# Attention with a mixture of experts: on VectorE, a tile's division moves behind the masked maxima of its tick, and the gate's bias is added one tick later

## The chip, the core and the metric

One program runs on one core of a Trainium2 chip. Its engines each work through their own list of instructions in order and wait for one another by semaphores: TensorE (PE in the rows; PEld is its weight load), VectorE (DVE), ScalarE (ACT), GpSimd (POOL) and SyncE (SP), which issues most DMAs. The metric is the device time of one execution in microseconds (us).

## The reference

The kernel computes block-sparse attention over 4 batches, 8 heads and 768 positions of 64 features, and then a mixture of 8 experts over the 3072 tokens that come out:

```python
scores = scale * np.matmul(q, k.transpose(0, 1, 3, 2))
# mask: neighbour blocks, first and last block, 3 sampled blocks a row of blocks
scores = np.where(mask, scores, -1000000000.0)
scores = scores - np.max(scores, axis=-1, keepdims=True)
attn = np.exp(scores)
attn = attn / (np.sum(attn, axis=-1, keepdims=True) + 1e-09)
...
logits = x @ w_gate + modality_bias[modality_id]
e_idx = np.argmax(logits, axis=1)
...
h = np.maximum(x[mask] @ w1[e], 0.0)
out[mask] = gate_w[mask, None] * (h @ w2[e])
```

## The kernel before

The work has two parts. The attention part (to about 226 us) makes 24 tiles of 128 token rows, `xr`; the experts' part multiplies groups of 256 rows that went to one expert, with every operand split into two fp32r halves, and keeps TensorE at it to the end.

A loop over ticks writes the attention part, and the program's order on every engine is the order in which this loop writes it. An item is a quarter of a sparse tile (two batches, two block rows of 32 queries), or a head pair of the dense first and last blocks ("d" items, which see all 768 keys). In tick `t` each step of `ORDER` is done for the item that is `LAG` ticks old:

- S: score products on TensorE (L557; dense L401), two PSUM banks that hold for two items
- M: masked maxima on VectorE, two custom instructions with a short read each (L565); dense: two plain maxima and a small one (L414 to L417)
- X: exponentials on ScalarE (L573; dense L423, L424)
- T and A: transposes on TensorE (L582; dense L433), copied out by ScalarE (L587; dense L440)
- W and V: products with the shared and with the own values (L604; L597 and L613), once a tile; dense L451
- O: `divide` on VectorE, once a tile, which reads V's two banks: add (L458), reciprocal (L459), multiply 128x512 (L460). It gives the tile's two banks back
- Y: transposes of the finished tile (L620), copied by ScalarE (L622)
- G: `gate`, the product with the gate's weights (L630), and on VectorE the add of the bias, `lg` (L633), behind which `end_tile` puts the routing of two tiles on a list, `fillers`

A sparse tile has four items, so TensorE's long steps fall on two ticks of four. Between the steps `hook(0)` to `hook(7)` take small work from lists: the routing (argmax, softmax weight, rank in the expert: L315 to L390, some 25 VectorE instructions of 0.15 to 0.25 us for two tiles), the choice of the first two groups, loads of the first experts' weights and their split (L752 on ScalarE, L755 on VectorE). The eight PSUM banks come from one pool. The line that matters:

```python
ORDER = 'OXTSMGVAYW'
```

So O is written first in its tick, ahead of M, and the bias is added in G's tick, right behind M.

Of the kernel before, what the change touches and what calls it, by code (L numbers as in the profile page):

```python
# [21 lines left out]
B, H, S, D = 4, 8, 768, 64  # L22
# [34 lines left out]
START_TICKS = 14  # L57
DENSE_DVE = ((0, 0), (0, 1))
DENSE_AFTER = (21, 29, 45, 47)
LAG = {'d': {'S': 0, 'M': 1, 'X': 2, 'T': 4, 'A': 4, 'W': 7, 'O': 8, 'V': 101, 'Y': 11, 'G': 13}, 's': {'S': 0, 'M': 1, 'X': 2, 'T': 4, 'A': 4, 'W': 5, 'V': 7, 'O': 8, 'Y': 10, 'G': 13}}  # L60
ORDER = 'OXTSMGVAYW'
ADVANCE = (((2, 3), (6, 6), (7, 1)), ((0, 2), (1, 1), (6, 4)))
LHS = (6, 5)
LHS_DVE = (True, True)
# [26 lines left out]
def attention_moe(ctx, tc, kD, qD, qH, v0, v1, blocks, modality, w_gate, bias, w1, w2, out):  # L91
# [30 lines left out]
    with ExitStack() as actx:  # L122
# [5 lines left out]
        def bank():  # L128
            return psum.tile([P, 512], F32, name="bank")
# [495 lines left out]
        def gate(tau, xT):  # L625
            tp = bank()
            for pr in range(NPAIR):
                for j in range(2):
                    r = slice(64 * j, 64 * j + 64)
                    nc.tensor.matmul(tp[r, 0:E], lhsT=xT[:, pr, r], rhs=wg_raw[:, pr, :], start=pr == 0, stop=pr == NPAIR - 1, tile_position=(0, 64 * j))  # L630
            if tau - tau % 2 not in lgs:
                lgs[tau - tau % 2] = small.tile([P, 2, E], F32, name="lg")
            nc.vector.tensor_tensor(lgs[tau - tau % 2][:, tau % 2, :], tp[:, 0:E], btok[:, tau, :], ALU.add)  # L633
# [596 lines left out]
        xrs, turns, banks, sums, ats, gated, written = {}, {}, {}, {}, {}, set(), {}  # L1230
# [5 lines left out]
        def tau_of(m, half):  # L1236
            return half * (NT // 2) + m + 1

        def end_tile(m, half):
            tau = tau_of(m, half)  # L1240
            gate(tau, turns.pop((m, half)))
            gated.add(tau)
            if tau ^ 1 in gated:
                t = tau - tau % 2
                fillers.append(routing(t, lgs.pop(t), [xrs.pop((t % (NT // 2) + n - 1, half)) for n in range(2)]))
# [9 lines left out]
        NI = len(items)  # L1255
# [6 lines left out]
        def hook(place):  # L1262
            for f in work_at.pop((t, place), []):
                f()
            if t < NI:
                ph = 0 if t < at["s", 1, 0, 0, 0] else 1
                for at_, k in ADVANCE[ph]:
                    if place == at_:
                        advance(k)
                for at_, k in CHOOSE:  # L1270
                    if place == at_:
                        step(choosers, k)
                for at_, k in EARLY:
                    if place == at_:
                        step(early, k)
                if place == LHS[ph] and slots_todo:
                    slot_lhs(nc.vector if LHS_DVE[ph] else nc.gpsimd)
# [41 lines left out]
        for g in range(2 * NM):  # L1319
            half, m = divmod(g, NM)  # L1320
            t = at["s", half, m, 0, 0]
# [21 lines left out]
        def do(op, it):  # L1343
            if (op, it) in done:
                return
            done.add((op, it))
            if it[0] == "d":
                _, b, pr = it
                half = b // HB
                if op == "S":  # L1350
                    if pr % 2 == 0:
                        for c, o in enumerate(dense_scores(b, pr)):
                            st["d", b, pr + c] = o
                elif op == "M":
                    st[it] = dense_max(b, pr, *st[it])
                elif op == "X":
                    st[it] = dense_exp(b, pr, *st[it])
                elif op == "T":
                    st[it] = dense_transpose(b, pr, *st[it])
                elif op == "A":  # L1360
                    st[it] = dense_copy(b, pr, *st[it])
                elif op == "W":
                    st[it] = dense_weigh(b, pr, *st[it])
                elif op == "O":
                    if (b % HB, pr) == (0, 0):
                        new_tile(-1, half)
                    dense_out(b, pr, *st.pop(it))
                elif (b % HB, pr) == (HB - 1, NPAIR - 1):
                    if op == "Y":
                        turns[-1, half] = turned(xrs[-1, half])  # L1370
                    elif op == "G":
                        end_tile(-1, half)
            else:
                _, half, m, n, b = it
                if op == "S":
                    if b == 0:
                        sp = scores(qraw[m, half], half * NM + m, n)
                        for b_ in range(HB):
                            st["s", half, m, n, b_] = sp
                elif op == "M":  # L1380
                    st[it] = masked(m, n, b, st[it])
                elif op == "X":
                    if (n, b) == (0, 0):
                        sums[m, half] = small.tile([P, 4, 2], F32, name="sums", bufs=4)
                    st[it] = exps(sums[m, half][:, 2 * b + n, :], *st[it])
                elif op == "T":
                    st[it] = transposed(n, st[it])
                elif op == "A":
                    if n == 0:
                        ats[m, half, b] = work.tile([P, 16, 2, 32], F32, name="at", bufs=NAT)  # L1390
                    copied(n, b, st.pop(it), ats[m, half, b])
                    if (n, b) == (1, HB - 1):
                        sums[m, half] = spread(sums[m, half])
                elif (n, b) == (1, HB - 1):
                    if op == "W":
                        st[it] = bank()
                        weigh_shared(half * NM + m, st[it], [ats[m, half, b_] for b_ in range(HB)])
                    elif op == "V":
                        banks[m, half] = bank()
                        sum_rows(sums.pop((m, half)), banks[m, half])  # L1400
                        weigh_own(half * NM + m, st[it], [ats[m, half, b_] for b_ in range(HB)])
                    elif op == "O":
                        new_tile(m, half)
                        divide(st.pop(it), banks.pop((m, half))[:, 0:H], slice(0, P), H, xrs[m, half][:, 0:HD])
                    elif op == "Y":
                        turns[m, half] = turned(xrs[m, half])
                    elif op == "G":
                        end_tile(m, half)

        man = tc.manual_schedule(engines=MAN) if MAN else ExitStack()  # L1410
        with man:
            constants()
            for token in START:
                op, at_ = token[0], tuple(int(c) for c in token[1:] if c.isdigit())
                if token[:2] == "SP":
                    spare(int(token[2:]))
                elif op == "h":
                    t = int(token[1:])
                    for spot in range(8):
                        hook(spot)  # L1420
                elif op.isupper():
                    do(op, ("d" if len(at_) == 2 else "s", *at_))
                elif token == "tb":
                    spare()
                else:
                    loads[token]()
            t = START_TICKS
            while t < NI + LAG["s"]["G"] + 1 or fillers or slots_todo or choosers or early:
                spot = 0
                for op in ORDER:  # L1430
                    if op in "TSMAXOW":
                        hook(spot)
                        spot += 1
                    for kind in "ds":
                        k = t - LAG[kind][op]
                        if 0 <= k < NI and items[k][0] == kind:
                            do(op, items[k])
                hook(7)
                if t >= NI:
                    tail[0], tail[1] = t >= NI + TAIL, t >= NI + LAG["s"]["V"]  # L1440
                    for _ in range(2):
                        advance(2)
                        while slots_todo:
                            slot_lhs(nc.vector if len(slots_todo) % 2 else nc.gpsimd)
                        step(choosers, 1)
                        step(early, 1)
                t += 1

        hp, op, xp = [bank() for _ in range(4)], [bank() for _ in range(2)], [bank() for _ in range(2)]
# [59 lines left out]
```

## Time and profile before

| | us |
|---|---|
| median of 3 runs (lowest, highest) | 521.74 (521.41, 523.24) |
| the profiled execution | 523.66 |
| its span, first to last instruction | 521.9 |
| TensorE busy in the span | 499.5 |
| VectorE, ScalarE, GpSimd busy | 388.4, 335.5, 244.9 |

The profiled execution is 1.9 us above the median, and its time 1.8 above its span. Busy times of TensorE are of pipelined instructions: of two neighbours the next begins some 0.07 us before the modelled end of the first, so an idle time that a row shows is somewhat shorter than the time lost.

### The profile page before, as it was taken

The numbers are of one execution on the slowest core, as the hardware profiler recorded it, in microseconds if no ns is written. First come the engines' busy times: TensorE is split into PE (matmuls) and PEld (weight loads), VectorE is DVE, ScalarE is ACT, GpSimd is POOL, SyncE is SP. The second block draws the span as 40 slices with busy tenths as digits, with TensorE's granted clock in tenths as the row PEclk, the third lists the DMA queues.
The fourth block names the chain that finished last, engine by engine and source line by source line (L and its number), as shares of the span: only waits on it lengthen the run. The fifth ranks groups of instructions, "written<-read, shape, count | busy, mean of one in ns | idle before, by whom it ended". The sixth has DMA issues, their size and how long they took to land.

```text
span 521.9 us, 18958 instructions
## 1 busy us (share of the span) xinstructions
PE 499.5 (96%) x7124; PEld 420.6 (81%) x7124; DVE 388.4 (74%) x1136; ACT 335.5 (64%) x765; POOL 244.9 (47%) x514
## 2 busy tenths in 40 slices
PE   7999999989899999899999999999999999999995
PEld 5667776767778777688989798998989899898974
DVE  5886688686689899967986868667686766768573
ACT  3799787978789978844545655555565545655561
POOL 6779685576458884312275051323324222241423
PEclk9999999999999999999999999999999999999999
DMA  8997885999756778965878797879669696877860
GB/s 293 332 249 227 241 222 184 244 228 258 196 174 191 207 219 245 273 192 200 242 281 294 246 297 258 266 233 301 200 240 284 227 295 202 280 223 251 260 209 25
DMA packets 59063, 123.84 MB, mean 237 GB/s; under 512 B 9681, under 2 KB 17618, under 8 KB 58962
## 3 DMA queue, kind: packets, MB, share of 16 engines
q1 hardware_dynamic: 54704, 108.88, 68.7%
q0 software_dynamic: 4256, 13.65, 7.9%
q8 instruction: 58, 0.95, 0.8%
q14 instruction: 43, 0.35, 0.3%
q10 hardware_dynamic: 2, 0.00, 0.0%
HBM read 105.97 MB, written 12.86 MB: 228 GB/s over the span
## 4 chain that ended last, share of the span: by engine, by line
PE 73%; DMA 11%; DVE 7%; ACT 3%; SPq 2%; issue 2%; POOL 0%; DVEq 0%; POOLq 0%; ACTq 0%
PE bank L810 8%; PE bank L812 8%; PE bank L811 8%; PE bank L827 7%; PE bank L826 7%; PE bank L825 7%; PE bank L557 6%; PE bank L582 6%; DMA slot<-x_d,gi 5%; PE bank L604 3%; PE bank L613 3%; PE bank L451 2%; DMA slot<-w 2%; PE bank L630 2%; PE bank L401 2%
## 5 line engine op out<-in xcount | busy, mean ns | idle before, releaser
L755 DVE TENSOR_TENSOR slot<-slot 128x1024 fp32r<-128x1024 f32 x99 | 124.6, 1272 | 63.1 <-ACT slot L752 54.9
L752 ACT CAST slot<-slot 128x1024 fp32r<-128x1024 f32 x104 | 107.0, 1047 | 68.3 <-PE bank L811 49.5
L810 PE MATMUL bank<-slot 128*128 128x256 f32 x384 | 108.4, 282 | 0.2 <-issue 0.2
L812 PE MATMUL bank<-slot 128*128 128x256 f32 x384 | 107.9, 281 | 0.1
L811 PE MATMUL bank<-slot 128*128 128x256 f32 x384 | 107.6, 280 | 0.0
L573 ACT ACTIVATE a<-y,mn 128x256 f32<-128x256 f32 x176 | 88.7, 511 | 7.9 <-DVE mn L565 7.7
L846 POOL DMA_INDIRECT out<-slot,si x20 | 27.3, 1364 | 109.5 <-ACT slot L842 106.5
L827 PE MATMUL bank<-slot 128*128 128x512 f32 x192 | 75.9, 395 | 0.4 <-DVE slot L818 0.4
L826 PE MATMUL bank<-slot 128*128 128x512 f32 x192 | 75.9, 395 | 0.0
L825 PE MATMUL bank<-slot 128*128 128x512 f32 x192 | 75.8, 395 | 0.0
L810 PEld LDWEIGHTS bank<-slot 128*128 128x128 f32 x384 | 72.3, 188 | 0.6
L811 PEld LDWEIGHTS bank<-slot 128*128 128x128 f32 x384 | 72.2, 188 | 0.6
L812 PEld LDWEIGHTS bank<-slot 128*128 128x128 f32 x384 | 72.2, 188 | 0.3 <-DVE slot L755 0.3
L565 DVE CUSTOM_DVE_ANT_1 y<-bank,smask 128x256 f32<-128x256 f32 x176 | 66.2, 416 | 0.5 <-PE bank L557 0.3
L502 POOL COPY slot<-slot 128x128 f32 x264 | 63.6, 293 | 0.0
L527 POOL TENSOR_SCALAR slot<-slot 32x1024 f32<-32x1024 f32 x40 | 41.7, 1042 | 33.2 <-issue 12.8
L587 ACT COPY at<-bank 128x512 f32<-128x512 f32 x88 | 50.6, 576 | 9.0 <-PE bank L582 9.0
L582 PE MATMUL bank<-ident,a 128*128 128x128 f32 x352 | 52.1, 280 | 3.0 <-issue 2.2
L557 PE MATMUL bank<-slot,q_raw 64*32 64x256 f32 x1408 | 48.7, 382 | 0.0
L582 PEld LDWEIGHTS bank<-ident,a 128*128 128x128 f32 x352 | 38.1, 141 | 7.3 <-issue 2.3
L827 PEld LDWEIGHTS bank<-slot 128*128 128x128 f32 x192 | 36.1, 188 | 9.2 <-DVE slot L818 0.9
L826 PEld LDWEIGHTS bank<-slot 128*128 128x128 f32 x192 | 36.0, 188 | 8.3 <-DVE slot L755 0.4
(307 smaller groups left out, 859.8 us busy)
## 6 DMA issues: line engine op xcount, KB each, us to landing
slot<-w SPq DMA_DIRECT2D x100, 512.0 KB, 5.2
slot<-v SPq DMA_DIRECT2D x180, 128.0 KB, 4.0
x_d<-xr SPq DMA_DIRECT2D x22, 256.5 KB, 4.2
q_raw<-qH SPq DMA_DIRECT2D x22, 256.0 KB, 4.8
slot<-v SPq DMA_DIRECT2D x16, 256.0 KB, 5.1
slot<-slot SPq DMA_DIRECT2D x120, 32.0 KB, 4.4
slot<-kD SPq DMA_DIRECT2D x13, 256.0 KB, 3.6
slot<-v SPq DMA_DIRECT2D x4, 768.0 KB, 12.4
```

The source lines that it names most:

```text
L557: nc.tensor.matmul(sp[u][32 * pr:32 * pr + 32, b * 256:(b + 1) * 256], lhsT=q[r, b * NPAIR + pr, n, :], rhs=kv[r, s0:s0 + 8, b, pr, :], st ...
L565: nc.vector.tensor_tensor_reduce(y[:, u, :].rearrange("p (s f) -> p s f", s=8), sp[u][:, b * 256:(b + 1) * 256].rearrange("p (s f) -> p s ...
L573: nc.scalar.activation(a[:, u, :], y[:, u, :], AF.Exp, bias=mn[:, u:u + 1], scale=-1.0, accum_out=total[:, u:u + 1])
L582: nc.tensor.transpose(tp[:, k:k + P], a[:, u, c * P:(c + 1) * P], ident)
L752: nc.scalar.copy(h, s)
L755: (eng or (nc.gpsimd if n in POOL_SPLITS else nc.vector)).tensor_tensor(l, s, h.bitcast(F32), ALU.subtract)
L810: nc.tensor.matmul(o, lhsT=h[:, fs], rhs=xh[g % 2][:, c, :], start=c == 0 and f % 2 == 0, stop=False)
L811: nc.tensor.matmul(o, lhsT=h[:, fs], rhs=xl[g % 2][:, c, :], start=False, stop=False)
L812: nc.tensor.matmul(o, lhsT=l[:, fs], rhs=xh[g % 2][:, c, :], start=False, stop=c == 3 and f % 2 == 1)
L825: nc.tensor.matmul(o, lhsT=hh[0][:, f, ts_], rhs=h[:, fs], start=f == 0, stop=False)
L826: nc.tensor.matmul(o, lhsT=hh[0][:, f, ts_], rhs=l[:, fs], start=False, stop=False)
L827: nc.tensor.matmul(o, lhsT=hl[f // 4][:, f % 4, ts_], rhs=h[:, fs], start=False, stop=f == 7)
```

## The change

O goes behind M in the tick's order. The gate's step is cut in two: G keeps the product, and a new step L, one tick older, adds the bias (in the last ticks, from `NI` on, L follows G at once). The hooks keep their places beside the other steps. The routing of a pair of tiles therefore starts one tick later.

```diff
-LAG = {'d': {'S': 0, 'M': 1, 'X': 2, 'T': 4, 'A': 4, 'W': 7, 'O': 8, 'V': 101, 'Y': 11, 'G': 13}, 's': {'S': 0, 'M': 1, 'X': 2, 'T': 4, 'A': 4, 'W': 5, 'V': 7, 'O': 8, 'Y': 10, 'G': 13}}
-ORDER = 'OXTSMGVAYW'
+LAG = {'d': {'S': 0, 'M': 1, 'X': 2, 'T': 4, 'A': 4, 'W': 7, 'O': 8, 'V': 101, 'Y': 11, 'G': 13, 'L': 14}, 's': {'S': 0, 'M': 1, 'X': 2, 'T': 4, 'A': 4, 'W': 5, 'V': 7, 'O': 8, 'Y': 10, 'G': 13, 'L': 14}}
+ORDER = 'XTSMLOGVAYW'
...
                     nc.tensor.matmul(tp[r, 0:E], lhsT=xT[:, pr, r], rhs=wg_raw[:, pr, :], start=pr == 0, stop=pr == NPAIR - 1, tile_position=(0, 64 * j))
+            return tp
+
+        def logits(tau, tp):
             if tau - tau % 2 not in lgs:
...
+        def gate_tile(m, half):
+            gates[m, half] = gate(tau_of(m, half), turns.pop((m, half)))
+
         def end_tile(m, half):
             tau = tau_of(m, half)
-            gate(tau, turns.pop((m, half)))
+            logits(tau, gates.pop((m, half)))
...
                     elif op == "G":
+                        gate_tile(m, half)
+                        if t >= NI:
+                            do("L", it)
+                    elif op == "L":
                         end_tile(m, half)
...
                 spot = 0
+                hook(spot)
                 for op in ORDER:
-                    if op in "TSMAXOW":
+                    if op in "TSMAXW":
+                        spot += 1
                         hook(spot)
-                        spot += 1
```

VectorE at the first tick of the loop in which a dense item's maxima stand with a division (62 to 67 us in the profile), before:

```order
L458 TENSOR_SCALAR rt<-bank 128x8
L459 RECIPROCAL rt<-rt 128x8
L460 TENSOR_TENSOR xr<-bank,rt 128x512
L414 TENSOR_REDUCE nm_1823<-bank 128x1
L415 TENSOR_REDUCE nm_1823<-bank 128x1
L417 TENSOR_SCALAR nb__1826<-nm_1823 128x1
L591 TENSOR_TENSOR rexp<-sums,quad 128x32
```

and with the change:

```order
L414 TENSOR_REDUCE nm_1818<-bank 128x1
L415 TENSOR_REDUCE nm_1818<-bank 128x1
L417 TENSOR_SCALAR nb__1821<-nm_1818 128x1
L458 TENSOR_SCALAR rt<-bank 128x8
L459 RECIPROCAL rt<-rt 128x8
L460 TENSOR_TENSOR xr<-bank,rt 128x512
L591 TENSOR_TENSOR rexp<-sums,quad 128x32
```

The division went behind the three instructions of the dense maxima. The second place is VectorE at the next such tick (84 to 89 us), before:

```order
L633 TENSOR_TENSOR lg<-bank,btok 128x8
L315 TENSOR_REDUCE mx<-lg 128x2
L458 TENSOR_SCALAR rt<-bank 128x8
L459 RECIPROCAL rt<-rt 128x8
L460 TENSOR_TENSOR xr<-bank,rt 128x512
L318 TENSOR_TENSOR dl<-lg,mx 128x16
L323 SCALAR_TENSOR_TENSOR eq<-dl,desc 128x16
L326 TENSOR_REDUCE first<-eq 128x2
L414 TENSOR_REDUCE nm_2425<-bank 128x1
L415 TENSOR_REDUCE nm_2425<-bank 128x1
L417 TENSOR_SCALAR nb__2428<-nm_2425 128x1
```

and with the change (L636 is the add of the bias):

```order
L414 TENSOR_REDUCE nm_2409<-bank 128x1
L415 TENSOR_REDUCE nm_2409<-bank 128x1
L417 TENSOR_SCALAR nb__2412<-nm_2409 128x1
L636 TENSOR_TENSOR lg<-bank,btok 128x8
L458 TENSOR_SCALAR rt<-bank 128x8
L459 RECIPROCAL rt<-rt 128x8
L460 TENSOR_TENSOR xr<-bank,rt 128x512
L591 TENSOR_TENSOR rexp<-sums,quad 128x32
L315 TENSOR_REDUCE mx<-lg 128x2
L318 TENSOR_TENSOR dl<-lg,mx 128x16
L323 SCALAR_TENSOR_TENSOR eq<-dl,desc 128x16
L326 TENSOR_REDUCE first<-eq 128x2
```

Here the maxima overtake the bias, the division and four instructions of the routing. The third place is VectorE near the end of the attention part (212 to 216 us), where the second group's rows are chosen (L1115 to L1122), before:

```order
L565 ISA mn 128x1
L1115 TENSOR_TENSOR hb<-oh,ce_5987 128x144
L1119 TENSOR_SCALAR off<-cm_5985,cm_5258 128x1
L1122 TENSOR_SCALAR rh__6105<-rhi,off 128x18
L458 TENSOR_SCALAR rt<-bank 128x8
L459 RECIPROCAL rt<-rt 128x8
L460 TENSOR_TENSOR xr<-bank,rt 128x512
L565 ISA y,mn<-bank,smask 128x256
```

and with the change:

```order
L565 ISA mn 128x1
L458 TENSOR_SCALAR rt<-bank 128x8
L459 RECIPROCAL rt<-rt 128x8
L460 TENSOR_TENSOR xr<-bank,rt 128x512
L591 TENSOR_TENSOR rexp<-sums,quad 128x32
L565 ISA y,mn<-bank,smask 128x256
```

The choice of rows, which now begins a tick later, no longer stands ahead of the last items' maxima.

## Rows read from the trace of the kernel before

**Rows 1.** Busy time by stretch: from:to, length, then PE, PEld, DVE, ACT, POOL (instructions), PEclk, DMA.

```profile
150.00:183.00 33.00, 33.00 (x918) 25.90 (x916) 29.34 (x145) 30.35 (x101) 26.43 (x80) 1.00 0.71 200
183.00:226.00 43.00, 39.44 (x1048) 31.21 (x1046) 38.82 (x191) 33.70 (x99) 21.86 (x43) 1.00 0.84 243
...
260.00:474.00 214.00, 213.57 (x1371) 193.09 (x1371) 153.12 (x188) 116.41 (x143) 72.50 (x79) 1.00 0.80 259
```

**Rows 2.** VectorE's waits, whole span: what waited, for whom, us, times, longest.

```profile
DVE rt L458 <- PE bank L597: 11.4, 8, 2.6
DVE lg L633 <- PE bank L630: 9.8, 12, 1.6
...
DVE xr L460 <- PE bank L613: 6.6, 13, 0.7
```

**Rows 3.** TensorE's groups, 30 to 226 us: busy, mean ns, idle before and who ended it.

```profile
L582 PE MATMUL bank<-ident,a 128*128 128x128 f32 x349 | 51.7, 280 | 3.0 <-issue 2.2 <-ACT a L423 0.5 <-ACT a L573 0.3
...
L604 PE MATMUL bank<-slot,at 128*64 128x64 f32 x704 | 26.8, 225 | 4.4 <-issue 2.9 <-ACT at L587 1.4
...
L451 PE MATMUL bank<-slot 128*64 128x64 f32 x240 | 9.0, 226 | 0.5 <-DVE mn L565 0.5
L433 PE MATMUL bank<-ident,a 128*128 128x128 f32 x48 | 7.2, 280 | 1.8 <-issue 1.5 <-ACT a L423 0.4
...
L597 PE MATMUL bank<-rexp,fold 128*32 128x8 f32 x176 | 5.5, 187 | 0.4 <-ACT at L587 0.4
```

**Rows 4.** Timeline of VectorE, first dense tick: start, length, instruction, idle before it.

```profile
63.68 0.17 DVE L458 TENSOR_SCALAR rt<-bank 128x8 f32<-128x8 f32 x1 [2.55 <-PE bank L597]
...
64.62 0.69 DVE L460 TENSOR_TENSOR xr<-bank,rt 128x512 f32<-128x512 f32 x1 [0.54 <-PE bank L613]
65.23 0.68 DVE L414 TENSOR_REDUCE nm<-bank 128x1 f32<-128x512 f32 x1
...
66.41 0.48 DVE L591 TENSOR_TENSOR rexp<-sums,quad 128x32 f32<-128x32 f32 x1
```

**Rows 5.** Timeline of ScalarE, same tick.

```profile
66.58 0.69 ACT L423 ACTIVATE a<-bank,nb__1826 128x512 f32<-128x512 f32 x1 [0.85 <-DVE nb__1826 L417]
```

**Rows 6.** Timeline of TensorE, same tick.

```profile
61.91 1.52 PE L401 MATMUL bank<-slot,qd 64*64 64x512 f32 x16
...
63.45 1.08 PE L613 MATMUL bank<-slot,at 128*32 128x64 f32 x64
...
65.48 1.09 PE L557 MATMUL bank<-slot,q_raw 64*32 64x256 f32 x32
...
67.46 0.94 PE L604 MATMUL bank<-slot,at 128*64 128x64 f32 x24 [0.32 <-issue]
```

**Rows 7.** Timeline of VectorE, second dense tick.

```profile
84.61 0.17 DVE L633 TENSOR_TENSOR lg<-bank,btok 128x8 f32<-128x8 f32 x1 [1.41 <-PE bank L630]
...
85.75 0.69 DVE L460 TENSOR_TENSOR xr<-bank,rt 128x512 f32<-128x512 f32 x1 [0.46 <-PE bank L613]
...
87.22 0.68 DVE L414 TENSOR_REDUCE nm<-bank 128x1 f32<-128x512 f32 x1
```

**Rows 8.** Timeline of TensorE, second dense tick.

```profile
89.40 0.66 PE L582 MATMUL bank<-ident,a 128*128 128x128 f32 x4 [0.54 <-ACT a L423]
...
91.36 0.44 PE L433 MATMUL bank<-ident,a 128*128 128x128 f32 x2 [0.37 <-ACT a L423]
```

**Rows 9.** Timeline of VectorE, one sparse tick: the maxima of an item and what follows.

```profile
180.00 0.41 DVE L565 CUSTOM_DVE_ANT_1 y<-bank,smask 128x256 f32<-128x256 f32 x1
...
180.68 0.21 DVE L591 TENSOR_TENSOR rexp<-sums,quad 128x32 f32<-128x32 f32 x1
```

**Rows 10.** Timeline of VectorE where the experts' part begins.

```profile
224.40 0.69 DVE L804 TENSOR_TENSOR slot<-bank,slot 128x512 fp32r<-128x512 f32 x1 [2.55 <-ACT slot L803]
...
228.59 2.35 DVE L755 TENSOR_TENSOR slot<-slot 128x1024 fp32r<-128x1024 f32 x2
```

**Rows 11.** Timeline of VectorE: two casts of one shape in the routing.

```profile
111.88 0.17 DVE L380 CAST rlo<-r 128x4 f32<-128x4 int32 x1
111.95 1.03 DVE L381 CAST rhi<-r 128x4 f32<-128x4 int32 x1
```

More of the change, by code (lines that the diff above doesn't have):

```diff
@@ L1237, in tau_of @@
             return half * (NT // 2) + m + 1
+        gates = {}
+        def gate_tile(m, half):
+            gates[m, half] = gate(tau_of(m, half), turns.pop((m, half)))
         def end_tile(m, half):
             tau = tau_of(m, half)
-            gate(tau, turns.pop((m, half)))
+            logits(tau, gates.pop((m, half)))
             gated.add(tau)
@@ L1371, in do @@
                     elif op == "G":
+                        gate_tile(-1, half)
+                    elif op == "L":
                         end_tile(-1, half)
@@ L1407, in do @@
                     elif op == "G":
+                        gate_tile(m, half)
+                        if t >= NI:
+                            do("L", it)
+                    elif op == "L":
                         end_tile(m, half)
```

## Prediction, made before the changed kernel ran

> **What bounds the kernel now.** I read the busy times by stretch first, because an average over the span hides that there are two parts. From 260 us on TensorE is busy 213.57 of 214 us; nothing that VectorE does there is changed, so a gain or loss can only be made before, and is carried to the end as it is. In the attention part TensorE is busy 33.00 of 33 us (150 to 183) and 39.44 of 43 (183 to 226), VectorE 29.34 and 38.82 [rows 1]: TensorE is the bound, with VectorE close behind it, closest in the second stretch.
>
> Then I read the waits of both engines. VectorE waits 11.4 us for V's sums before the division, 6.6 us for V's products inside it and 9.8 us for the gate's product before the bias, 27.8 us in all [rows 2]. That is what the change goes at, and most of it is worth nothing: while VectorE waits there, TensorE works. What can be won is TensorE's own idle time, 30 to 226 us. Of it, 6.6 us in the rows shown have only "issue" as releaser, which no order on VectorE touches; 3.5 us end with an instruction of ScalarE or VectorE (0.5 and 0.3 at L582, 1.4 at L604, 0.5 at L451, 0.4 at L433, 0.4 at L597) [rows 3]. These 3.5 us, with what "issue" hides of the same cause, are the ceiling.
>
> **The change part by part.** No instruction is added or removed; it is a matter of who stands behind whom.
>
> *Dense ticks.* Last I read the three ticks in which dense maxima meet a division. In the first, VectorE stands idle 2.55 us, begins the division at 63.68, waits 0.54 us more inside it, and only then, at 65.23, begins the maxima, though the dense products ended at 61.91 + 1.52 = 63.43 [rows 4, 6]. ScalarE waits 0.85 us for the maxima and exponentiates at 66.58 [rows 5]; TensorE's W, at 67.46, has 0.32 us of idle before it [rows 6]. The row says "issue", but W begins 0.2 us behind the first exponential's end (66.58 + 0.69 = 67.27), which I take to be the reader of the bank that W writes. The third such tick (120 to 126) repeats this with 0.30 us. In the second, bias, division and routing all stand ahead, the maxima begin at 87.22, and TensorE loses 0.54 and 0.37 us to the exponentials [rows 7, 8]. With the maxima first, the exponentials come 1.6 us earlier or more, which is over every one of these gaps: 0.32 + 0.30 + 0.54 + 0.37 = 1.5 us, bounds 0.9 (the two gaps named by the rows) and 1.5.
>
> *The other waits named.* The 0.5 us at L451 wait for maxima behind a long piece of the rank's work, which now starts a tick later: I take it whole, bounds 0 and 0.5. The rest, 1.4 + 0.4 + 0.3 = 2.1 us [rows 3], lies mostly between 183 and 226 us, where VectorE has no slack. There the maxima now overtake a division (1.2 us from L458 to the next instruction when it needn't wait: 65.23 - 63.68 less 0.54, and some 0.2) and, for the last items, the choice of the second group's rows. But ScalarE's copies also stand behind its own weight casts, which stay. I take half, 1.0, bounds 0 and 2.1. Since an idle row is shorter than the time lost by some 0.1 us, six gaps gone give 0.6 more (bounds 0 and 0.8). Gain: 1.5 + 0.5 + 1.0 + 0.6 = 3.6 us.
>
> *What is late next: the division.* In a sparse tick the maxima take 180.68 - 180.00 = 0.68 us [rows 9], then 0.4 us of small instructions stand before the multiply. V on TensorE lasts 1.08 [rows 6], and the maxima's scores are done before V begins: the maxima fit into the wait for V, and the division ends as now, or up to 0.3 us later. This cover is worth nothing where VectorE is already late (183 to 226), and there TensorE's next need of the two banks decides. In a dense tick the cover is short: the dense maxima take 66.41 - 65.23 = 1.18 us. From 63.43 they end at 64.6, the small instructions at 65.0, the multiply at 65.7; now it ends at 64.62 + 0.69 = 65.31, and the score products S, whose second bank is the division's in the built program before and after, begin at 65.48, 0.17 us behind it [rows 4, 6]. So S is held some 0.4 us, twice (bounds: 0, if the first maximum may start before the last dense product, and 0.65, if it starts 0.25 late). In the second tick the maxima end between 85.3 and 85.8, as their products are done before the 84.61 of the bias [rows 7]; the multiply starts between 85.75 and 86.2: 0.2 us, bounds 0 and 0.45. Loss 1.0, bounds 0 and 1.75.
>
> *The bias one tick later.* What waits behind it on VectorE is only the routing, 20 to 30 small instructions a pair of tiles that nobody needs soon. The gate's bank is held a tick longer; the pool gives it out later for that, and the built program has its next user over 2 us of TensorE's work away. On SyncE's queue four stores of finished rows move a tile later and the halves of the first weights a tick later; on GpSimd's the gathers keep their place ahead of the same work. Their cover is that five buffers of rows go round; without it a division would wait for a store to land. Cost 0, bounds 0 and 0.5.
>
> *The start of the experts.* From 224.40 to the weights' splits at 228.59, VectorE runs without a gap behind its 2.55 us wait [rows 10], and TensorE soon needs the first of these splits. With the routing later, a few of its instructions move from ahead of 224 into this stretch: 0.3 us, bounds 0 and 0.6 (seven small instructions).
>
> **Sum.** 3.6 - 1.0 - 0.3 = 2.3 us less: the profiled execution's 523.66 (span 521.9) would become 521.3. It lay 1.9 us above the median of the timed runs; the same 2.3 us off the median 521.74 give **519.4 us**. With the bounds of the terms it is 516.8 (gains 4.9, no loss) to 523.7 (gains 0.9, losses 2.85).
>
> **A rule weighed.** Two casts of one shape, next to each other, take 0.17 and 1.03 us [rows 11], so the routing's small instructions can cost six times their usual, and a tick's shift changes which of them do. The Trainium skill (SBUF — State Buffer, "Who interferes with whom") says that VectorE's copies, casts and tensor-scalars can need a port pair that GpSimd shares, and that the second to issue is blocked for the whole of the other's instruction. By the row alone the shift costs nothing on average; by the rule it could put such an instruction ahead of maxima that were free of it, which is the last rival.
>
> **The rivals.**
> *Nothing is won* (521.0 to 522.5): the removed gaps come back. For it: TensorE has 6.6 us of idle that nobody named releases, S held by the division takes up to 1.75, and only 3.5 us were there to win. Against it: three ticks show the maxima late by a wait that the new order cannot have.
> *The stretch of 183 to 226 is VectorE's* (517): all 3.5 us and the hidden 0.8 go and S is not held, 4.3 to 4.9 us less. For it: VectorE's 38.82 of 43 us there. Against it: ScalarE's casts.
> *Slower, by the division's banks*: if the dense maxima cannot start before VectorE's division would now have ended, S waits the whole 1.18 - 0.17 = 1.0 us in three ticks, and where VectorE is late each of some six tiles from 183 to 226 gives its banks back 0.68 us later, against a TensorE that I give no slack there: 3.0 + 4.1, less the 3.6 gained: 525.2. It decides once divisions end over 0.2 us later than now in the dense ticks and over half a microsecond in the late ones. For it: the 0.17 us of [rows 4, 6]; against it: in two of the three ticks VectorE stands idle before.
> *The collisions*: the shift makes five rounds of late routing longer by 0.9 us each (1.03 less 0.17), half of it felt by TensorE: 2.2 us, so 521.6.
>
> **Chances.** My forecast (517.8 to 520.8) 0.50; nothing won 0.20; VectorE's stretch 0.13; slower by the banks 0.10; collisions 0.07. A measurement of this kernel tells about 0.5% (2.6 us) from no change. Below 519.1: a little under half of the forecast and all of the third, 0.36. Above 524.4: the fourth case, 0.10. Within: 0.54. The range is 517.0 to 523.0: below it lies about half of the third case, above it the fourth and little else.
>
> **What the changed profile would show.** Right: VectorE's waits for V and for the gate fall from 27.8 us to under 15; in the three dense ticks the dense maxima begin within 0.3 us of the dense products' end and W and the transposes after them have no gap; TensorE's idle time named for ScalarE and VectorE falls from 3.5 to about 1.5 us, with new idle at S (L557) of under 1.5. Wrong: idle at S over 2 us, VectorE's waits moved to the maxima instead of gone, TensorE's start into the experts (first L810) not about 2 us earlier, or other "issue" gaps than now, which would move the time by as much as the whole forecast without a cause in the change.

## The result, and the profile after

The changed kernel took **529.18 us**, the median of 6 runs (525.1 to 531.4), against 521.70 of 6 runs of the kernel before on the same chip. The ratio on record is 1.0101, 95% interval 1.0063 to 1.0139; the two medians by themselves stand at 1.0143. So it is slower by 1% or somewhat more, where 519.4 was forecast with a range of 517.0 to 523.0. On a second chip it was 528.43 against 523.98 (1.0083, 1.0049 to 1.0118); the kernel before differs by up to 4.5 us between chips, so only kernels of one chip are compared below. Ratios and means leave out the runs that are more than 1.5% above the fastest of their kernel: 5 of 12 in the second measurement of the division alone, 9 of 35 of the kernel before on one chip, 4 of 35 or fewer elsewhere.

The profiled execution took 525.1 us (span 523.4). It is the fastest of the six and only 1.4 us above the profiled execution of the kernel before; a second profile, of a run of 529.81 us, follows under the experiments. The busy times of the first by stretch, to be read against [rows 1] (the last number is what the DMA engines moved, in GB/s):

```profile
150.00:183.00 33.00, 32.45 (x898) 25.67 (x900) 27.71 (x132) 28.68 (x96) 25.85 (x71) 1.00 0.72 203
183.00:226.00 43.00, 37.93 (x974) 29.62 (x954) 35.71 (x183) 31.20 (x93) 19.81 (x41) 0.96 0.85 232
...
260.00:474.00 214.00, 213.17 (x1391) 192.49 (x1391) 155.74 (x190) 115.76 (x142) 72.77 (x79) 1.00 0.78 255
```

From 260 us on TensorE is as busy as before. From 183 to 226 TensorE is busy 1.5 us less, VectorE 3.1 us less, and the granted clock is 0.96 on average where it was 1.00.

VectorE's waits, against [rows 2], and TensorE's between 30 and 226 us, against [rows 3]:

```profile
DVE y L565 <- ACT a L573: 8.7, 6, 3.4
DVE r L363 <- PE bank L353: 8.6, 7, 3.0
...
DVE y L565 <- PE bank L557: 5.8, 6, 2.2
...
DVE xr L460 <- PE bank L613: 1.5, 4, 0.5
...
DVE lg L636 <- PE bank L630: 0.7, 1, 0.7
```

```profile
PE bank L604 <- issue: 2.8, 3, 2.3
PE bank L433 <- issue: 2.8, 1, 2.8
PE bank L604 <- POOL slot L488: 1.1, 1, 1.1
PE bank L604 <- ACT at L587: 0.6, 2, 0.4
PE bank L613 <- issue: 0.6, 1, 0.6
PE bank L557 <- DVE lg L636: 0.5, 1, 0.5
PE bank L582 <- DVE rt L458: 0.5, 1, 0.5
PE bank L582 <- ACT a L573: 0.4, 1, 0.4
PE bank L1147 <- DVE hoh L1137: 0.4, 1, 0.4
PE bank L620 <- DVE xr L460: 0.4, 1, 0.4
PE bank L620 <- DVE mn L565: 0.2, 1, 0.2
```

The waits for V and the gate, 27.8 us, are down to 2.2 (1.5 + 0.7): the edit does what it says. But VectorE now waits at the maxima instead (8.7 + 5.8) and at the rank (8.6); it is ahead, and ScalarE and TensorE set its pace. TensorE's idle time that an engine's name ends went from 3.5 to 4.1 us. The "issue" idle time hardly changed as a sum, 7.1 before (2.9 + 2.2 + 1.5 + 0.5) and 6.4 now with the row of 0.2 that is left out, but two stops of 2.8 and 2.3 us make up most of it.

The timelines of the first dense tick, VectorE's first dense maxima and then TensorE, show the gain that was forecast, against [rows 4] and [rows 6]:

```profile
61.33 0.69 DVE L414 TENSOR_REDUCE nm<-bank 128x1 f32<-128x512 f32 x1 [2.33 <-PE bank L401]
```

```profile
60.21 1.52 PE L401 MATMUL bank<-slot,qd 64*64 64x512 f32 x16
...
63.78 1.09 PE L557 MATMUL bank<-slot,q_raw 64*32 64x256 f32 x32
64.80 0.64 PE L630 MATMUL bank<-wg_raw,xT 128*64 128x8 f32 x16
65.29 1.52 PE L604 MATMUL bank<-slot,at 128*64 128x64 f32 x32
```

The maxima begin at 61.33, 0.4 us before the dense products end (60.21 + 1.52 = 61.73). S is not held and W has no idle time before it. TensorE is 1.70 us ahead of the kernel before at the dense products (61.91 less 60.21) and 2.17 at W, so the tick itself gives 0.47 us. The 1.70 are no gain of this tick: 0.79 of them are there at 11 us already, behind the waits for the first loads, and most of the rest is a stop of 0.81 us at 52 us that only the kernel before has. The second dense tick, and then the kernel before at the same instructions:

```profile
86.37 0.66 PE L582 MATMUL bank<-ident,a 128*128 128x128 f32 x4
86.87 0.60 PE L620 MATMUL bank<-ident,xr 128*128 128x128 f32 x4
87.30 0.99 PE L433 MATMUL bank<-ident,a 128*128 128x128 f32 x6
...
89.95 1.08 PE L613 MATMUL bank<-slot,at 128*32 128x64 f32 x64
93.82 0.88 PE L433 MATMUL bank<-ident,a 128*128 128x128 f32 x6 [2.79 <-issue]
```

```profile
92.92 1.08 PE L613 MATMUL bank<-slot,at 128*32 128x64 f32 x64
93.93 0.88 PE L433 MATMUL bank<-ident,a 128*128 128x128 f32 x6
...
220.42 0.94 PE L604 MATMUL bank<-slot,at 128*64 128x64 f32 x18
222.48 0.63 PE L604 MATMUL bank<-slot,at 128*64 128x64 f32 x14 [1.12 <-issue]
223.04 1.09 PE L797 MATMUL bank<-ident,slot 128*128 128x128 f32 x8
...
226.22 0.38 PE L810 MATMUL bank<-slot 128*128 128x256 f32 x1
```

The gaps of 0.54 and 0.37 us [rows 8] are gone and TensorE is 2.97 us ahead at L613 (92.92 less 89.95), 0.80 more than at the first tick's W. One instruction group later it is ahead by 0.11: it stood still for 2.79 us with "issue" as the only releaser. The same happens where the attention ends. The timeline of the changed kernel, and its busy time and clock in short stretches there:

```profile
219.19 0.66 PE L604 MATMUL bank<-slot,at 128*64 128x64 f32 x15
222.16 0.81 PE L604 MATMUL bank<-slot,at 128*64 128x64 f32 x17 [2.31 <-issue]
222.90 1.97 PE L800 MATMUL bank<-ident,slot 128*128 128x128 f32 x8
...
226.88 0.39 PE L813 MATMUL bank<-slot 128*128 128x256 f32 x1
```

```profile
215.90:219.80 3.90, 3.46 (x130) 3.17 (x130) 3.63 (x17) 2.94 (x9) 0.00 (x0) 1.00 1.00 274
219.80:222.10 2.30, 0.04 (x1) 0.00 (x0) 0.44 (x5) 0.00 (x0) 0.00 (x0) 1.00 1.04 290
222.10:222.60 0.50, 0.44 (x15) 0.44 (x16) 0.00 (x0) 0.00 (x0) 0.00 (x0) 0.98 0.94 250
222.60:226.00 3.40, 3.40 (x42) 2.95 (x39) 1.28 (x8) 1.35 (x3) 0.20 (x1) 0.50 0.48 164
226.00:230.00 4.00, 4.00 (x100) 3.75 (x92) 3.77 (x24) 2.50 (x4) 2.57 (x3) 1.00 0.15 34
```

TensorE was 1.23 us ahead at this W (220.42 less 219.19), stood 2.31 us where the kernel before stands 1.12, and was 0.32 ahead behind it. Then the granted clock is 0.50, that is 1.2 of 2.4 GHz, for 3.4 us, and eight transposes take 1.97 us instead of 1.09. The experts begin at 226.88 instead of 226.22.

**What these stops are.** The profile page's row "q8 instruction: 58, 0.95, 0.8%" has the packets that bring TensorE's instructions: 58 of 16 KB. Count TensorE's rows (matmuls, weight loads, its sequencer's own) in order of time, from 0, and the first one behind every "issue" stop over 0.4 us has a number that leaves 193 or 194 when divided by 256: 1986, 5058, 5825 and 10433 in the kernel before, 4034, 7873 and 10433 in the changed one. TensorE gets its program in pieces of 256 instructions, and stops where a piece ends and the next has not come. The DMA queues show the fetch to the second stop, from 215.9 to 219.6 us without a row of q8, and from 219.6 to 219.7:

```profile
q1 hardware_dynamic: 223, 0.53, 54.7%
q0 software_dynamic: 140, 0.47, 43.6%
```

```profile
q8 instruction: 1, 0.02, 73.2%
...
```

Its packet begins 3.7 us behind the last piece's end (215.92), and 2.5 us later TensorE goes on. In the median over a profile's first 42 pieces a fetch begins 1.3 to 1.8 us behind that end, by the packets' times.

**Clock and rest.** What the clock takes from a run is estimated as (1 - granted clock) x span of its row. The estimate is rough: in all 18 profiles the clock falls to 0.50 once more at the end, behind TensorE's last matmul (in the kernel before at 519.93 us, where that matmul ends at 515.5). That costs TensorE nothing, but it puts 0.35 to 2.2 us of a run into the column "of it clock" and takes as much out of "rest". Means against the kernel before on the same chip, in us:

| kernel | difference | of it clock | rest |
|---|---|---|---|
| the kernel before, measured again | +0.84 | +0.50 | +0.34 |
| whole change | +4.50 | +1.71 | +2.79 |
| division alone, twice | +1.40, -1.10 | +1.58, -0.10 | -0.18, -1.00 |
| bias alone | +4.81 | +2.49 | +2.32 |
| whole change, 13 tiny matmuls less | +5.25 | +2.40 | +2.85 |
| bias late, tiles 1-11 / 13-17 / 18-19 | -0.60 / +1.75 / +1.69 | -0.76 / +1.05 / -0.61 | +0.16 / +0.70 / +2.30 |
| whole change, 18-19 in time | +3.31 | +1.99 | +1.32 |
| twelve loads less: change / before | +0.31 / -1.50 | +0.89 / -0.19 | -0.58 / -1.31 |
| six loads of group 7 less: change | +4.78 | +1.67 | +3.11 |
| all eighteen less: change / before / 18-19 in time | -0.06 / -2.24 / -1.76 | -0.70 / -1.30 / -0.64 | +0.64 / -0.94 / -1.12 |

A ratio has an interval of some 0.35% to either side, 1.8 us; the table is read with that.

### The profile page after: what moved, and what is told of

It is laid out like the page before. It is cut to its first block, busy times and chain, and to the rows that moved or that the text cites. A ratio compares the mean times of both kernels' runs of the same rounds, so it can differ in the third digit from the quotient of the medians.

```text
span 523.4 us, 18981 instructions
## 1 busy us (share of the span) xinstructions
PE 501.0 (96%) x7124; PEld 421.5 (81%) x7124; DVE 387.8 (74%) x1136; ACT 335.4 (64%) x765; POOL 246.3 (47%) x514
## 4 chain that ended last, share of the span: by engine, by line
PE 64%; DVE 12%; DMA 10%; issue 5%; ACT 3%; POOL 2%; SPq 2%; POOLq 1%; DVEq 0%; ACTq 0%
PE bank L830 6%; PE bank L829 6%; PE bank L828 6%; PE bank L815 6%; PE bank L813 6%; PE bank L814 6%; PE bank L557 6%; PE bank L582 6%; DMA slot<-x_d,gi 5%; DVE slot L758 3%; DMA slot<-w 3%; PE bank L604 3%; PE bank L613 2%; PE bank L451 2%; PE bank L401 2%
## 5 line engine op out<-in xcount | busy, mean ns | idle before, releaser
L813 PE MATMUL bank<-slot 128*128 128x256 f32 x384 | 108.2, 282 | 0.0
L565 DVE CUSTOM_DVE_ANT_1 y<-bank,smask 128x256 f32<-128x256 f32 x176 | 66.5, 417 | 16.1 <-ACT a L573 8.7
L815 PEld LDWEIGHTS bank<-slot 128*128 128x128 f32 x384 | 72.2, 188 | 0.7 <-DVE slot L758 0.7
L813 PEld LDWEIGHTS bank<-slot 128*128 128x128 f32 x384 | 72.2, 188 | 0.6
L814 PEld LDWEIGHTS bank<-slot 128*128 128x128 f32 x384 | 72.2, 188 | 0.4
L557 PE MATMUL bank<-slot,q_raw 64*32 64x256 f32 x1408 | 50.2, 382 | 0.5 <-DVE lg L636 0.5
L830 PEld LDWEIGHTS bank<-slot 128*128 128x128 f32 x192 | 36.1, 188 | 10.2 <-DVE slot L821 1.9
L829 PEld LDWEIGHTS bank<-slot 128*128 128x128 f32 x192 | 36.0, 188 | 7.9
L828 PEld LDWEIGHTS bank<-slot 128*128 128x128 f32 x192 | 36.1, 188 | 7.7
## 6 DMA issues: line engine op xcount, KB each, us to landing
slot<-v SPq DMA_DIRECT2D x4, 768.0 KB, 13.8
```

The lines of the kernel that those rows point to most:

```text
L557: nc.tensor.matmul(sp[u][32 * pr:32 * pr + 32, b * 256:(b + 1) * 256], lhsT=q[r, b * NPAIR + pr, n, :], rhs=kv[r, s0:s0 + 8, b, pr, :], st ...
L565: nc.vector.tensor_tensor_reduce(y[:, u, :].rearrange("p (s f) -> p s f", s=8), sp[u][:, b * 256:(b + 1) * 256].rearrange("p (s f) -> p s ...
L813: nc.tensor.matmul(o, lhsT=h[:, fs], rhs=xh[g % 2][:, c, :], start=c == 0 and f % 2 == 0, stop=False)
L814: nc.tensor.matmul(o, lhsT=h[:, fs], rhs=xl[g % 2][:, c, :], start=False, stop=False)
L815: nc.tensor.matmul(o, lhsT=l[:, fs], rhs=xh[g % 2][:, c, :], start=False, stop=c == 3 and f % 2 == 1)
L828: nc.tensor.matmul(o, lhsT=hh[0][:, f, ts_], rhs=h[:, fs], start=f == 0, stop=False)
```

## The experiments

**The whole change, a half at a time.** The theory from the two traces (F) is that of the stops at piece ends; the rival (B) is the one priced ahead, late divisions that hold banks. The changed kernel again; the division alone; the bias alone; and a kernel in which all piece ends fall elsewhere:

```
divide_only: ORDER = 'XTSMOGVAYW', end_tile(m, half) right behind gate_tile(m, half)
bias_only:   ORDER = 'OXTSMLGVAYW'
after_gap4:  WARM_GAP = 4   (17 before)
```

> The changed kernel once more, for a second profile and more times. Theory F (TensorE stops at the ends of its pieces of 256 instructions until the next 16 KB piece has been fetched, and a long stop costs the clock as well): 526 to 531 us; in 30 to 230 us the idle time of TensorE that ends at nothing the profile shows is 7 us or more, and besides the end at least one stretch has a granted clock of 0.5, right behind such a stop. Theory B (divisions and bias that come late hold banks): the same time, but the waits of TensorE named for the division, the logits and the copies of VectorE between 100 and 226 us are 5 us or more and longer than in the first profile, and the clock stays at 1.0 before 500 us.

528.43 us (1.0083). Its stops of 2.5 and 3.9 us are at the same two instructions as in the first profile, and each has the clock behind it. Columns as above, the first stop and what follows, then the second:

```profile
92.40:94.70 2.30, 0.00 (x0) 0.00 (x0) 1.74 (x6) 0.77 (x4) 2.08 (x2) 1.00 0.88 247
95.20:98.50 3.30, 3.30 (x41) 1.95 (x39) 0.00 (x0) 2.85 (x10) 0.00 (x0) 0.50 0.83 235
222.50:224.80 2.30, 0.00 (x0) 0.00 (x0) 0.07 (x2) 0.00 (x0) 0.00 (x0) 1.00 1.04 237
224.90:231.70 6.80, 5.43 (x97) 4.98 (x99) 2.53 (x16) 1.84 (x4) 0.81 (x1) 0.50 0.64 172
```

TensorE's waits named for the division's and the bias's banks are 0.4 us each. F holds here, B does not.

> The division behind the masked maxima, the bias in the gate's own tick as before. Theory B: the waits at the divisions' banks are the loss, so 525 or more. Theory F: which piece ends fall on dense work decides, not the division; nothing says that it must be slow: 519 to 527, with VectorE's waits at the matmuls of the weights (27.8 us before) below 18 all the same.

524.67 us, 1.0025 (0.9984 to 1.0067); VectorE's waits for V are gone from the top rows, with 16.1 us left at the bias. The division costs nothing that can be measured, and wins nothing.

> The bias one tick later, the division ahead of the maxima as before. Theory B: no division is late, so 521 to 523. Theory F: 520 to 527, by where the stops fall; VectorE's waits at the division, the logits and the copy of the gate stay above 20 us.

528.18 us, 1.0102 (1.0068 to 1.0136): the loss is the bias's. No division is late here, so the price that was put on late divisions is not what is paid.

> The changed kernel with 13 tiny matmuls (32 by 16) less at its start, where TensorE has 1.5 us of idle time: all later instructions of TensorE stand 26 places earlier in the pieces of 256, and nothing else changes. Theory F: the stops move to other instructions, and the time changes by more than 1.5 us, most likely down, to 520 to 526, since by the first profile fewer of the ends of pieces then follow less than 4.4 us on the one before (3.7 us of shortfall in all where there were 6.1). Theory B: banks and engines are as they were, so 527 to 531 and the same waits.

528.62 us, 1.0104 (1.0049 to 1.0158). The stops did move: 1.84 us before L557 at 207 and 1.17 before L613 at 215, again at numbers that leave 193 and 194. But the time did not move with them: F gave more than 1.5 us, most likely down, and that was wrong, so my count of short pieces said nothing about it. At the end of the attention this kernel waits 2.41 us for the early gathers instead.

> The division behind the masked maxima alone, once more, for an interval. If the division costs nothing, the ratio to the kernel before is 0.998 to 1.004, and VectorE's waits for the matmuls of the weights are again below 18 us.

0.9964 (0.9919 to 1.0008), with 13.8 us at the bias; together with the first time, no difference that can be measured. Its 12 runs lie far apart (520.2 to 533.9 us); the mean of all of them is 1.3 us above that of all 35 of the kernel before, 2.0 of it clock by the estimate and -0.7 rest.

**Which tiles' bias.** The bias is late for some tiles only, with the division as before:

```
if t >= NI or not (tau_of(m, half) >= 18):      # bias_end; < 13: bias_first; 13 to 17: bias_mid
    end_tile(m, half)
```

> The division ahead of the maxima as before; the bias is one tick late for the tiles 18 and 19 alone (and for the two dense tiles 0 and 12), which come last before the ticks that have no attention scores left. Theory R (the late bias of the last pair puts the routing one tick's seven steps behind at the end, so that its last rank waits behind VectorE's work for the experts, and the stop of TensorE at the experts' start grows): all of the loss of the late bias is here, +3 to +5 us on the kernel before; from the last matmul of the gate to the last rank 6.3 us where the kernel before has 4.2. Theory W (the late bias costs a little wherever a tile has it, by banks and by waits of VectorE): within 1 us of the kernel before.

> The division as before; the bias one tick late for the tiles 1 to 11 alone (and 0 and 12). Theory R: within 1 us of the kernel before, 4.2 us from the last matmul of the gate to the last rank. Theory W: +2 us or more, since half of the tiles have it.

> The division as before; the bias one tick late for the tiles 13 to 17 alone (and 0 and 12). Theory R: within 1 us of the kernel before. Theory W: +1 to +2 us.

> The changed kernel, but with the bias of the tiles 18 and 19 in their own gate's tick; the division behind the maxima. Theory R: the loss is gone, 524 to 525 where the kernel before has 524 (as with the division moved alone), 4.2 us from the last gate to the last rank. Theory W: 527 or more, as with the whole change.

526.61 us (1.0030, 1.0000 to 1.0060), 525.56 (0.9984, 0.9948 to 1.0020), 526.81 (1.0046, 1.0012 to 1.0079) and 530.14 (1.0059, 1.0022 to 1.0096). By these alone neither theory holds. Without the clock's part R has the place right: the rest is 2.30, 0.16 and 0.70 us, and 2.32 for all tiles. It has not the size: bias_end costs 1.69 us in all, not 3 to 5, and the three parts add up to 2.84 us where the bias of all tiles costs 4.81. From the last gate to the last rank are 6.35 us in bias_end, 4.22 in the three others. TensorE's row for that rank in bias_end, then in bias_mid:

```profile
246.79 0.18 PE L353 MATMUL bank<-oh,onesb 128*128 128x16 bf16 x1 [0.80 <-DVE oh L328]
```

```profile
243.81 0.18 PE L353 MATMUL bank<-oh,onesb 128*128 128x16 bf16 x1 [0.20 <-DVE oh L328]
```

VectorE's timeline in the changed kernel shows why: the rank's one-hot of the last pair (L328) stands behind one more multiplication for the experts (L821), which waits for ScalarE. In the kernel before it follows L326 by 0.21 us (239.57 and 239.78).

```profile
241.06 0.17 DVE L326 TENSOR_REDUCE first<-eq 128x2 f32<-128x16 f32 x1
242.03 0.69 DVE L821 SCALAR_TENSOR_TENSOR slot<-bank,slot 128x512 fp32r<-128x512 f32 x1 [0.81 <-ACT slot L820]
242.64 0.17 DVE L328 TENSOR_TENSOR oh<-desc,first 128x16 bf16<-128x16 f32 x1
```

What this costs can be read from the profiles. From the last matmul of the gate to the 400th matmul from the end, TensorE takes 215.2 to 216.1 us in the eight profiles in which the last pair's bias is late, and 214.0 to 215.1 in the ten others: 1.2 us between the means, with 1.2 to 1.8 us of idle time in it against 0.2 to 0.9.

after_end_now is late by the clock (1.99 of its 3.31 us): stops of 2.79 and 2.31 us at the old places, the clock at 0.50 behind each.

**Is it the loads?** Where the attention ends the DMA engines are full (1.00 and 1.04 in the stretches above). Loads of own rows left out, in both kernels, so that these groups compute with older rows:

```
if g >= 2 * NM - 2:          # twelve loads; == 7: six; in (7, 20, 21): eighteen
    return
```

> The changed kernel without the twelve loads of own v rows (128 KB each, issued between 206 and 220 us) of the last two groups, which then compute with older rows. Theory D (where the attention's scores end, the DMAs are the bound: own v, the early gathers and TensorE's next piece of instructions land at 220 to 227 us whatever the engines do, so what TensorE gained before is spent standing there, and the longer stop lowers the clock): TensorE's longest stop in 215 to 230 us is below 1 us, the granted clock is 1.0 from 210 to 240 us, and the time is 4 us or more below the changed kernel's, 520 to 524 where the kernel before has 524 to 526. Theory P (the piece end falls on dense work, and its fetch is late whatever else is moved): the stop at that piece end stays above 2 us, and the time falls by less than 1.5 us.

> The kernel before without the same twelve loads. Theory D: 1 to 4 us below the kernel before, and the changed kernel without these loads is then within 1 us of this one. Theory P: within 1.5 us of the kernel before, and the changed kernel without the loads stays 3 us or more above this one.

525.96 us (1.0010, 0.9979 to 1.0041) and 524.71 (0.9958, 0.9930 to 0.9986). The stop at the experts' start is gone: the longest from 215 to 230 us is 1.4, and not a fetch:

```profile
PE bank L817 <- DVE slot L760: 1.4, 1, 1.4
```

The clock is 1.00 there, while the stop at 94 us (3.06) and the clock behind it are as before. The fetch begins 1.4 to 2.0 us behind its piece's end here in the five profiles without these loads, and 3.7 to 5.9 in the four of the changed order that have them and the stop. The two kernels are now 1.8 us apart (0.31 + 1.50 in the table) instead of 4.5, where D gave at most 1 and P at least 3. D holds for this stop; what that is worth is some 2.7 us, with 1 us or more of uncertainty.

> The changed kernel without the six loads of own rows of group 7 alone (issued at 87 to 90 us), which then computes with older rows. Theory D (loads ahead of the fetch hold TensorE up): its stop between 90 and 98 us falls from 2.5 to 3.1 us to under 1 us, the granted clock is 1.0 from 90 to 110 us, the stop at 219 to 227 us stays above 2 us, and the time is 1 to 4 us below the changed kernel's (4 to 5 us above the kernel before). Theory Q (the piece end is late for a reason of TensorE's own, loads or not): the stop stays above 2 us.

529.07 us, 1.0077 (1.0043 to 1.0111). The stop at 94 us is down to 1.69, with ScalarE's exponential as the releaser that the profile names, and no clock falls there. But its fetch still begins 4.2 us behind the piece's end, and the time is as it was: the other stop was 4.25 us long, with the clock behind it. For this stop D holds in half at most.

> The changed kernel without the loads of own rows of groups 7, 20 and 21. Theory D: neither of the two long stops is there, no clock below 1.0 before 500 us, and the time is within 0.5% of the same reduction of the kernel before. Theory Q: as after_less_dma, with the stop at 94 us and a clock of 0.5 behind it, 1 us or more above the reduced kernel before.

> The kernel before without the same loads, to compare with. It has no long stop at 94 us: 0 to 3 us below the kernel before.

> As after_no_3, but with the bias of the tiles 18 and 19 in their own gate's tick, so that the routing at the end is not late. If the late routing is what is left of the loss: 1 to 2.5 us below after_no_3, at or below before_no_3, with 4.2 us from the last gate to the last rank. If it is not: as after_no_3.

524.95 us (0.9974, 0.9939 to 1.0009), 522.69 (0.9956, 0.9916 to 0.9997) and 523.22 (0.9963, 0.9924 to 1.0002). Without the loads the change costs 2.2 us (0.06 less than 2.24), and with the last routing in time 0.5 (2.24 less 1.76). after_no_3 still has a stop of 1.42 us at 94 and one of 1.40 at 228, with the clock at 0.50 behind the second, so "no clock below 1.0" was wrong. The 2.2 us fit what D allowed (0.5%) and what Q gave (1 us or more).

> The kernel before, for a second profile. If stops at piece ends and the clock behind them explain the times of both kernels, a run of 524 us or more shows TensorE's stops above 7 us in all or a stretch at a granted clock of 0.5 before 500 us, and a run of 522 us or less shows neither. If not, it is another cause.

526.94 us, 1.0010. The profiled run took 526.03 with 7.5 us of stops at piece ends, none over 2.18, and a clock of 1.00 up to the end, as far as that goes: the kernel before stops as much in all, only never as long.

## Why the prediction was wrong, step by step

*Carried to the end as it is:* right. From 260 to 474 us TensorE is busy 213.17 us of 214, before 213.57.

*Dense ticks, 1.5 us gained:* right as a mechanism. The maxima begin 0.4 us before their products' end, W and the transposes lose their gaps, S is not held; the first such tick gives TensorE 0.47 us and the stretch from there to behind the second 0.80. *The division late, 1.0:* wrong in its place. It was forecast at S in the dense ticks, where nothing is lost, because the maxima do start before the last dense product, the case for which the prediction gave 0. TensorE's idle time that ends with the division is 0.5 + 0.4 us at 214 and 215 us, where the sum had no figure, so the agreement in size is luck; and the division alone costs nothing that can be measured. *Other named waits, 1.0 gained:* wrong; all named waits are 4.1 us where 3.5 were, with GpSimd's copy (1.1 at L604) and the bias (0.5 at L557) new among them. That VectorE's waits moved to the maxima was one of the signs of being wrong that the prediction named.

*The step that failed first* is "6.6 us in the rows shown have only 'issue' as releaser, which no order on VectorE touches". The sum stayed (7.1 and 6.4), but these are waits for a fetch that goes its own way: TensorE came 2.97 us earlier to one and left it 0.11 us earlier, 1.23 earlier to another and left it 0.32 earlier. A gain ahead of a fetch that is late is given back there. The prediction even named "other 'issue' gaps than now" as what would make it wrong, but put no term on it; the rival "nothing is won" (0.20) leans on these 6.6 us, and ends at no change.

*The second* is the bias: "Cost 0, bounds 0 and 0.5", because the routing is something "that nobody needs soon". In the middle that is so (0.16 us for tiles 1 to 11). At the end it enters the last ticks a tick late, and the last rank waits behind the experts' work: 1.2 us by the profiles, 1.7 by the times (2.2 less 0.5 without the loads), 1.69 by bias_end.

*What had no term at all* is TensorE's clock. By the estimate above its part of the whole change is 1.7 us on one chip. On the first, where the one profiled run of the kernel before has 0.998 and the six of the changed one 0.984 to 0.993, it is (1 - 0.998) x 521.9 = 1.0 us against 5.98 in the mean of the six runs, so 4.9 of some 7 us; with one run on one side this is a rough figure.

*The start of the experts, 0.3:* mis-sized. The first L813 is 0.66 us later (226.88 less 226.22) instead of 2 us earlier, from the stop and the clock.

*The rivals.* "Slower, by the division's banks" has the sign and, at 525.2, about half of the size here, by a cause that the division alone refutes. "The stretch of 183 to 226 is VectorE's" fails with the named waits, which did not go. "The collisions" are not seen: the casts at L380 and L381 take at most 0.38 us in the changed kernel's profile, where one took 1.03 before.

So of 4.5 us some 2.3 (4.5 less 2.2) hang on the loads that meet the fetch at the end of the attention, with the clock behind it, 1.2 to 1.7 on the late routing, and the remainder is too little to tell. Each of these differences of times is uncertain by 1 us or more, and they come from different chips. Shown is that the loss comes with the late bias and not with the division, and that the stop there goes when the loads go. Not shown is how a late bias of the tiles before the last pair makes the loss of all tiles larger than the sum of its parts. Not settled is why the fetch to the stop at 94 us begins 4.2 to 6.0 us behind its piece's end in all eight profiles with both parts of the change, and 0.7 to 1.9 in the ten others: six loads explain a part of its length, not its lateness. The loss does not need that stop: the bias alone has none at 94 us and costs 4.81 us. A version that beats the kernel before was not found.

## What to carry to other kernels

Before you add up idle time, find out what "issue" is: if its places are a fixed number of instructions apart, it is a fetch, and time won ahead of it is worth nothing when the fetch is late all the same. Price a delay at the place where its chain ends, not where it is long: a tick that nobody misses in a loop is missed by the last turn. And where TensorE already stops for 2 us, a longer stop can be paid twice, once as idle time and once as clock.

## What the runs showed of the hardware

**Instruction fetch.** Pieces are 256 instructions of 16 KB in all; at a stop of over 0.4 us its packet has ended 1.2 to 1.9 us before TensorE goes on (2.1 once), and 4.7 to 10.7 us of a run stood still so in 16 of 18 profiles (3.1 and 2.1 us in the kernel before without loads). The Trainium skill (Runtime: NRT & Kernel Launch, "Instruction fetch mechanics") gives the same 16 KiB and 256 instructions and calls the cost of crossing such a boundary "mostly hidden". The trace agrees on the size. On the cost it agrees for most crossings: in the kernel before 5 of 38 between 30 and 226 us have an "issue" stop of over 0.3 us. But what is not hidden adds up to 6.2 of the 7.1 us of "issue" idle time there.

**The clock.** In the 18 profiles, from 30 us on, the granted clock fell to 0.50 (1.2 of 2.4 GHz) twenty times before TensorE's last matmul, always in or within 2 us of a stop of TensorE of 1.35 us or more, for 3 to 7 us. Of 13 stops over 2.2 us 12 had such a fall with or behind them, and the one of 2.79 us at 94 us in the changed kernel's first profile had none; of 24 from 1.3 to 2.2 us, 8 had. The kernel before, with stops of up to 2.18 us there, had none in two profiles.
